# Causal mixing and a gated projection in token blocks: blocks taken in pairs, the second with its stages in reverse order

## The chip, the cores and the metric

The kernel runs on one core of one Trainium2 chip. The metric is the device time of one execution in microseconds; before the change it is 393.89 us, the median of three runs (393.89 to 394.47).

## The reference

`x` is 8 sequences of 4224 tokens with 192 channels. In the first step each of 8 heads (24 channels each) is a causal sum over 7 tokens, with softmaxed weights. The second step computes, on the result, a gate (a causal convolution over 5 tokens for each channel, then a sigmoid) and a value (a 192 x 192 projection), multiplies them, and projects again with 192 x 192 weights:

```python
w = softmax(weight)                                  # (8, 7), per head
x1[s] = sum_k w[h, k] * x[s - 6 + k]                 # head h of each channel
gate = sigmoid(sum_k conv_w[k] * x1[s - 4 + k])      # 5 taps per channel
out = (gate * (x1 @ w_val)) @ w_out                  # (8, 4224, 192), float32
```

## The kernel before

The tokens are worked on in two halves side by side. Channels lie on partitions: 128 of the 192 channels of each half fill one tile part `x1` (two halves, index q = 0 and 1), and the 64 channels left over of both halves together fill 128 partitions of `x2`.

*Superblocks and convolution units.* 14 superblocks (groups) of 2, 3 or 5 windows hold the tokens. The first step is a matmul with a band matrix. `conv_unit` does four windows of it into one PSUM bank (`pc`, line 310), ACT evicts the bank to `e` (line 319), and `scatter` sends it by DMA into `x1` and `x2` of the group. There are 114 units, and units for a group run two groups ahead. `todo[n]` says how many run with block n: 5 in blocks 3 and 4, then 4, 3, 3 repeating, 2 in each of the blocks 26 to 31, none later.

*Blocks.* The second step goes by blocks of 302 to 502 tokens per half; there are 36, of 448 columns (blocks 2 to 7, 32 and 33) or 502 (blocks 8 to 31), with smaller ones at both ends. For a block n:

- the gate: `gate_open` (ACT, line 382) writes the first tap into PSUM, `gate_taps` (DVE, line 389) adds the four others, and `gate_close` (ACT, line 402) writes the sigmoid to SBUF. Part 0 (`pa`, the 128 channels, two banks) and part 1 (`pb`, the 64 left over, one bank) are separate. The sigmoids go to `g1` and `g2`, with two buffers each.
- `split` (x) and `split_gated1`, `split_gated2` (the product): ACT casts to a rounded high part, POOL subtracts it to get a low part (lines 410, 411 for part 1, 418, 419 for part 2).
- the projections `v` and `o`, each into three banks: q = 0, 1 for the 128 channels of each half, 2 for the 64 of both. `diagonal` (line 445) and `main` (line 455) use the whole 128 x 128 array, `columns` (line 483) uses 128 x 64 tiles in f32, `rows` (line 468) uses 64 x 128 tiles. Products are written as three matmuls of high and low parts, except in `columns`.
- `gated` (DVE, line 502) multiplies v's bank by the gate, in place in `g1` or `g2`; `project` (ACT, line 518) evicts o's bank, and after the last one the block is sent out by DMA.

*The order.* It is written out by hand: each engine executes its instructions in the order of the program text. The loop over n does the v projection of block n, the o projection of block n - 1, most of the gate of n + 1 and the opening of the gate of n + 2, in the order `diagonal` v and o, `main` v, `columns` v and o, `rows` v and o, `main` o, and then the units of `todo[n]`.

*PSUM.* Of eight banks `pa` has two, `pb` one, and five rotate among `pc`, `v` and `o`.

Of the kernel before, what the change touches and what calls it, by code (L numbers as in the profile page):

```python
# [7 lines left out]
F32 = mybir.dt.float32  # L8
# [5 lines left out]
PSUM = bass.MemoryType.PSUM  # L14
# [3 lines left out]
NH, KW, HC, KG = 8, 7, 24, 5  # L18
# [50 lines left out]
STEPS = []  # L69
# [5 lines left out]
N = len(STEPS)  # L75
# [16 lines left out]
LAG = 2  # L92
BY_POOL, EARLY, AHEAD = 3, 4, 6
WARM = 11, 5, 14

SOON = {2: (0, 2), 3: (1, 3), 4: (3, 5), 5: (5, 8)}


@with_exitstack
def kernel(  # L100
# [9 lines left out]
    nc = tc.nc  # L110
# [6 lines left out]
    pp = ctx.enter_context(tc.tile_pool(name="pp", bufs=2))  # L117
    op = ctx.enter_context(tc.tile_pool(name="op", bufs=3))
    ps_g = ctx.enter_context(tc.tile_pool(name="ps_g", bufs=1, space=PSUM))
    ps_h = ctx.enter_context(tc.tile_pool(name="ps_h", bufs=1, space=PSUM))  # L120
    ps = ctx.enter_context(tc.tile_pool(name="ps", bufs=5, space=PSUM))
    ctx.enter_context(
        tc.manual_schedule(engines={ENG.PE, ENG.Activation, ENG.DVE, ENG.Pool, ENG.SP})
    )

    loads = []
    o = 0
    for g, n in enumerate(NJS):  # L130
        k = PER_LOAD[n]
# [20 lines left out]
    def load_x(upto):  # L152
        while loaded[0] < min(upto, len(loads)):
            i = loaded[0]
            loaded[0] += 1
            g, hs, o = loads[i]
            f = len(hs) * NJS[g] * M
            t = xtiles[i] = xin.tile([WK, XW], F32, tag="x", name=f"x_{i}")
            nc.sync.dma_start(t[:, :f], xw[o : o + WK * f].rearrange("(p f) -> p f", f=f))
# [13 lines left out]
    def scratch(n, i):  # L173
        o = scr_at[i]
        scr_at[i] += n
        return scr[i][:, o : o + n].bitcast(I32)

    raw = {}
    for name, ap, n, i in (("wv", wv, 2 * D + 2 * KG, 2), ("wo", wo, 2 * D, 1)):
        t = scratch(2 * n, i)  # L180
# [16 lines left out]
    nc.scalar.activation(warm, one, AF.Exp)  # L197

    def zeros(k):
        pw = ps.tile([128, 512], F32, tag="p", name="pw")  # L200
        for i in range(k):
            nc.tensor.matmul(pw[:M, :WIN], lhsT=zero[:, :M], rhs=zero[:, M:], start=True, stop=True)

# [90 lines left out]
    first_unit = [next(i for i, u in enumerate(units) if u[0] == g) for g in range(NG)] + [len(units)]  # L294

    def conv_unit(u):
        g, q, ws = units[u]
        n = NJS[g]
        if u == first_unit[g]:
            x1s[g] = xp.tile([128, 2 * XB], F32, tag="x1", name=f"x1_{g}")  # L300
            x2s[g] = xp.tile([128, XC], F32, tag="x2", name=f"x2_{g}")
        if ws[0] == (0, 0):
            es[g, q] = ep.tile([M, 4 * NMAX * WIN], F32, tag="e", name=f"e_{g}_{q}")
        e = es[g, q]
        pc = ps.tile([128, 512], F32, tag="p", name=f"pc_{u}")
        for k, (hi, j) in enumerate(ws):
            h = QUADS[q][hi]
            i, at = home[g, h]
            c = (at * n + j) * M
            nc.tensor.matmul(  # L310
                pc[:M, k * WIN : (k + 1) * WIN],
                lhsT=xtiles[i][:, c : c + M],
                rhs=band[:, 4 * q + hi, :],
                start=True,
                stop=True,
            )
        a = (ws[0][0] * n + ws[0][1]) * WIN
        w = len(ws) * WIN
        nc.scalar.copy(e[:, a : a + w], pc[:M, :w])  # L319
        done = [hi for hi, j in ws if j == n - 1]  # L320
        for hi in done:
            h = QUADS[q][hi]
            i, at = home[g, h]
            last = at == len(loads[i][1]) - 1
            if last and g >= BY_POOL:
                load_x(allowed(i))
            scatter(g, h, e[:, hi * n * WIN : (hi + 1) * n * WIN])
            if last and g < BY_POOL:
                load_x(allowed(i))
# [40 lines left out]

    accs, g1s, g2s, xs, pr, ots, banks = {}, {}, {}, {}, {}, {}, {}

    def gate_open(n, i):
        if n >= N:
            return
        m = STEPS[n][2]
        if i == 0:
            acc = ps_g.tile([128, 2, 512], F32, tag="pa", name=f"pa_{n}")[:, :, :m]
        else:
            acc = ps_h.tile([128, 512], F32, tag="pb", name=f"pb_{n}")[:, :m]  # L380
        accs[n, i] = acc
        nc.scalar.mul(acc, views(n, 0)[i], cwt[:, i, 0:1])  # L382

    def gate_taps(n, i, k0=1, k1=KG):
        if n >= N:
            return
        acc = accs[n, i]
        for k in range(k0, k1):
            nc.vector.scalar_tensor_tensor(  # L389
                out=acc, in0=views(n, k)[i], scalar=cwt[:, i, k : k + 1],  # L390
                in1=acc, op0=ALU.mult, op1=ALU.add,
            )

    def gate_close(n, i):
        if n >= N:
            return
        m = STEPS[n][2]
        if i == 0:
            dst = g1s[n] = gp.tile([128, 2, MB], F32, tag="g1", name=f"g1_{n}")[:, :, :m]
        else:  # L400
            dst = g2s[n] = gp.tile([128, MB], F32, tag="g2", name=f"g2_{n}")[:, :m]
        nc.scalar.activation(dst, accs.pop((n, i)), AF.Sigmoid)  # L402

# [16 lines left out]
    HALVES = (slice(0, 64), slice(64, 128))  # L422

    def bank(what, n, q):
        t = ps.tile([128, 512], F32, tag="p", name=f"{what}_{n}_{q}")[:, : STEPS[n][2]]
        banks[what, n, q] = t
        return t

    def operands(what, n):
        return (w_val, *xs[n, 1], *xs[n, 2]) if what == "v" else (w_out, *pr[n, 1], *pr[n, 2])  # L430
# [4 lines left out]
    def ok(n):  # L435
        return 0 <= n < N

    def diagonal(what, n):
        if not ok(n):
            return  # L440
        acc = bank(what, n, 2)
        w, _, _, h2, l2 = operands(what, n)
        r = slice(W22, W22 + 128)
        for i, (a, b) in enumerate(parts(w, h2, l2)):
            nc.tensor.matmul(acc, lhsT=a[:, r], rhs=b, start=(i == 0), stop=False)  # L445

    def main(what, n, q):
        if not ok(n):
# [23 lines left out]
    def columns(what, n):  # L472
        if not ok(n):
            return
        m = STEPS[n][2]
        acc = banks[what, n, 2]
        w = w_val if what == "v" else w_out
        x = views(n)[0] if what == "v" else g1s[n]
        cuts = [m * i // 4 for i in range(5)]
        for i in range(4):  # L480
            c = slice(cuts[i], cuts[i + 1])
            for q, p in enumerate(HALVES):
                nc.tensor.matmul(  # L483
                    acc[p, c], lhsT=w.f[:, W12 : W12 + 64], rhs=x[:, q, c],
                    start=False, stop=(i == 3),
                )

    def split(n):
# [9 lines left out]
    def gated(n, q):  # L498
        if not ok(n):
            return  # L500
        v = g1s[n][:, q] if q < 2 else g2s[n]
        nc.vector.tensor_tensor(out=v, in0=banks.pop(("v", n, q)), in1=v, op=ALU.mult)  # L502

    def split_gated1(n):
        if ok(n):
# [6 lines left out]
    def project(n, q):  # L512
        if not ok(n):
            return
        m = STEPS[n][2]
        if n not in ots:
            ots[n] = op.tile([128, 3 * MB], F32, tag="ot", name=f"ot_{n}")
        nc.scalar.copy(ots[n][:, q * m : (q + 1) * m], banks.pop(("o", n, q)))  # L518
        o = 3 * sum(s[2] for s in STEPS[:n])
        if n == LAST:  # L520
            nc.sync.dma_start(out[:, o + q * m : o + (q + 1) * m], ots[n][:, q * m : (q + 1) * m])
        elif q == 1:
            nc.sync.dma_start(out[:, o : o + 3 * m], ots[n][:, : 3 * m])
# [7 lines left out]
    done = [0]  # L531

    def conv(k):
        for _ in range(k):
            if done[0] < len(units):
                conv_unit(done[0])
                done[0] += 1

    todo = [0] * (N + 1)
    for g in range(LAG, NG):  # L540
        a, b = SOON.get(g) or (first[g - LAG], first[g - 1])
        k = first_unit[g + 1] - first_unit[g]
# [15 lines left out]
    split(0)  # L558
    w_out.join(nc.gpsimd)
    gate_taps(0, 0)  # L560
    conv(1)
    gate_close(0, 0)
    gate_open(1, 0)
    w_out.cast(nc.gpsimd)
    conv(first_unit[LAG] - done[0])
    gate_taps(0, 1)
    gate_close(0, 1)
    gate_open(1, 1)

    for n in range(N + 1):  # L570
        diagonal("v", n)
        gate_taps(n + 1, 0, 1, 3)
        split(n + 1)
        diagonal("o", n - 1)
        main("v", n, 0)
        main("v", n, 1)
        gate_taps(n + 1, 0, 3, KG)
        columns("v", n)
        gated(n, 2)
        gate_close(n + 1, 0)  # L580
        gate_open(n + 2, 0)
        columns("o", n - 1)
        split_gated2(n)
        project(n - 1, 2)
        rows("v", n)
        gated(n, 0)
        gated(n, 1)
        rows("o", n - 1)
        split_gated1(n)
        main("o", n - 1, 0)  # L590
        gate_taps(n + 1, 1)
        project(n - 1, 0)
        main("o", n - 1, 1)
        project(n - 1, 1)
        conv(todo[n])
        gate_close(n + 1, 1)
        gate_open(n + 2, 1)


# [89 lines left out]
```

## Time and profile before

| | |
|---|---|
| median of three runs | 393.89 us |
| the profiled execution's own time | 394.33 us |
| its span (first to last instruction) | 392.5 us |
| mean granted TensorE clock | 0.994 |
| PE busy | 377.6 us (96%) |
| DVE busy | 342.6 us (87%) |
| ACT busy | 323.3 us (82%) |
| POOL busy | 255.0 us (65%) |

PE is the matmuls, PEld the weight loads that overlap them, DVE the vector engine, ACT the scalar engine, POOL the GpSimd engine, SP the engine that issues most DMAs. In rows of instructions the columns are start and duration in us, engine, line, operation, output and inputs, shapes, count, and in brackets the idle time before and what ended it. A row with a count covers several instructions in sequence, so its duration is that of all of them. In rows of waits the columns are the engine that waits, whom for, total us, number of waits, longest.

### The profile page before, as it was taken

To read this page: it belongs to the slowest core of one execution; us is meant where nothing else is said; L and a number is where in the kernel's file an instruction comes from. 1 tells how busy PE (TensorE), PEld (TensorE's weight loads), DVE (VectorE), ACT (ScalarE), POOL (GpSimd) and SP (SyncE) were. 2 spreads that over 40 slices of the span, in tenths; PEclk is the share of its full clock that TensorE was granted. 3 is DMA by queue.
4 is the path that set the end of the run, shared out by engine and by line. 5 is a ranking of instruction groups with operands and counts; after the bars stand their busy time and mean duration, and the time that the engine had idled before them with its cause. 6 is when DMAs were issued, how large, how long until landed. Compare 5 with 4: busy or idle time off the path is not lost.

```text
span 392.5 us, 8623 instructions
## 1 busy us (share of the span) xinstructions
PE 377.6 (96%) x3204; PEld 320.5 (82%) x3204; DVE 342.6 (87%) x424; ACT 323.3 (82%) x525; POOL 255.0 (65%) x177
## 2 busy tenths in 40 slices
PE   8977999999999999999999999999999999999895
PEld 7965989988888888888888888888888777788684
DVE  3798798887998998998999899899899999999970
ACT  7467888978988888888889888888888888887863
POOL 1876865566666665666665676666566776766771
PEclk9998999999999999999999999999999999999999
DMA  8866769998888687867867758768887644334224
GB/s 294 243 167 200 216 199 300 225 270 247 259 249 218 206 261 229 234 201 242 234 193 245 223 193 256 211 193 264 248 233 218 219 151 154 114 123 144 80 90 160
DMA packets 38209, 82.49 MB, mean 210 GB/s; under 512 B 4856, under 2 KB 17528, under 8 KB 38168
## 3 DMA queue, kind: packets, MB, share of 16 engines
q1 hardware_dynamic: 36720, 79.90, 66.7%
q0 software_dynamic: 896, 1.31, 1.5%
q10 hardware_dynamic: 552, 0.73, 0.6%
q8 instruction: 25, 0.41, 0.5%
q14 instruction: 16, 0.13, 0.1%
HBM read 29.34 MB, written 26.00 MB: 141 GB/s over the span
## 4 chain that ended last, share of the span: by engine, by line
PE 71%; DVE 11%; DMA 6%; ACT 5%; POOL 2%; issue 2%; SPq 1%; ACTq 0%; DVEq 0%; POOLq 0%
PE pc L310 18%; PE o L455 10%; PE v L455 9%; PE v L483 7%; PE v L468 6%; PE o L483 6%; DVE pa L389 5%; PE o L468 5%; PE o L445 5%; PE v L445 4%; DVE pb L389 3%; DMA x<-xw 2%; DMA x<-e 2%; DVE g L502 2%; DMA scr<-wv 2%
## 5 line engine op out<-in xcount | busy, mean ns | idle before, releaser
L389 DVE SCALAR_TENSOR_TENSOR pa<-x,cwt,pa 128x1004 f32<-128x1004 f32 (+5 forms) x144 | 172.9, 1201 | 7.2 <-ACT pa L382 2.2
L411 POOL TENSOR_TENSOR xl<-x,xh 128x1004 fp32r<-128x1004 f32 (+5 forms) x36 | 74.8, 2077 | 73.9 <-ACT xh L410 65.3
L310 PEld LDWEIGHTS pc<-band,x 128*120 128x120 f32 x912 | 101.1, 184 | 7.1 <-ACT e L319 1.4
L310 PE MATMUL pc<-band,x 128*120 128x122 f32 x912 | 102.7, 269 | 3.5 <-DMA x<-xw 1.9
L389 DVE SCALAR_TENSOR_TENSOR pb<-x,cwt,pb 128x502 f32<-128x502 f32 (+5 forms) x144 | 102.3, 710 | 3.8
L502 DVE TENSOR_TENSOR g<-v,g 128x502 f32<-128x502 f32 (+5 forms) x108 | 65.9, 643 | 24.7 <-PE v L468 17.0
L411 POOL TENSOR_TENSOR pl<-g,ph 128x1004 fp32r<-128x1004 f32 (+5 forms) x36 | 79.3, 2204 | 9.1 <-ACT ph L410 6.8
L402 ACT ACTIVATE g<-pa 128x1004 f32<-128x1004 f32 (+5 forms) x36 | 34.5, 958 | 42.8 <-DVE pa L389 22.7
L419 POOL TENSOR_TENSOR pl<-g,ph 128x502 fp32r<-128x502 f32 (+5 forms) x36 | 42.9, 1191 | 38.0 <-ACT ph L418 38.0
L319 ACT COPY e<-pc 120x488 f32<-120x488 f32 x114 | 58.8, 588 | 3.6 <-PE pc L310 3.4
L518 ACT COPY ot<-o 128x502 f32<-128x502 f32 (+5 forms) x108 | 55.9, 551 | 1.5 <-PE o L455 1.0
L382 ACT ACTIVATE pa<-x,cwt 128x1004 f32<-128x1004 f32 (+5 forms) x36 | 37.8, 1050 | 8.3 <-DMA x<-e 6.2
L419 POOL TENSOR_TENSOR xl<-x,xh 128x502 fp32r<-128x502 f32 (+5 forms) x36 | 41.8, 1162 | 0.0
L483 PEld LDWEIGHTS v<-x,wvf 128*64 128x64 f32 x576 | 29.4, 138 | 11.9 <-issue 11.3
L483 PE MATMUL v<-x,wvf 128*64 128x125 f32 (+4 forms) x576 | 37.5, 272 | 0.0
L410 ACT CAST ph<-g 128x1004 fp32r<-128x1004 f32 (+5 forms) x36 | 35.1, 976 | 1.5 <-DVE g L502 1.5
L483 PE MATMUL o<-g,wof 128*64 128x125 f32 (+4 forms) x576 | 35.6, 264 | 0.0
L410 ACT CAST xh<-x 128x1004 fp32r<-128x1004 f32 (+5 forms) x36 | 34.6, 962 | 0.0
L483 PEld LDWEIGHTS o<-g,wof 128*64 128x64 f32 x576 | 30.9, 136 | 0.1
L455 PE MATMUL o<-ph,woh 128*128 128x502 f32 (+5 forms) x72 | 30.8, 428 | 0.0
L455 PE MATMUL v<-xl,wvh 128*128 128x502 f32 (+5 forms) x72 | 27.4, 381 | 0.8 <-POOL xl L411 0.8
L455 PE MATMUL v<-xh,wvl 128*128 128x502 f32 (+5 forms) x72 | 27.4, 381 | 0.0
(75 smaller groups left out, 572.4 us busy)
## 6 DMA issues: line engine op xcount, KB each, us to landing
x<-xw SPq DMA_DIRECT2D x64, 300.0 KB
out<-ot SPq DMA_DIRECT2D x24, 753.0 KB
x<-e SPq DMA_DIRECT2D x40, 285.9 KB
x<-xw SPq DMA_DIRECT2D x20, 360.0 KB
out<-ot SPq DMA_DIRECT2D x8, 672.0 KB
x<-e SPq DMA_DIRECT2D x32, 141.6 KB
x<-e SPq DMA_DIRECT2D x25, 171.6 KB
x<-e SPq DMA_DIRECT2D x16, 94.4 KB
```

Of the source, the lines that this page charges most:

```text
L310: nc.tensor.matmul(pc[:M, k * WIN : (k + 1) * WIN], lhsT=xtiles[i][:, c : c + M], rhs=band[:, 4 * q + hi, :], start=True, stop=True,)
L319: nc.scalar.copy(e[:, a : a + w], pc[:M, :w])
L382: nc.scalar.mul(acc, views(n, 0)[i], cwt[:, i, 0:1])
L389: nc.vector.scalar_tensor_tensor(out=acc, in0=views(n, k)[i], scalar=cwt[:, i, k : k + 1], in1=acc, op0=ALU.mult, op1=ALU.add,)
L410: nc.scalar.copy(h, x)
L411: nc.gpsimd.tensor_tensor(out=l, in0=x, in1=h.bitcast(F32), op=ALU.subtract)
L419: nc.gpsimd.tensor_tensor(out=l, in0=x, in1=h.bitcast(F32), op=ALU.subtract)
L455: nc.tensor.matmul(acc, lhsT=a[:, r], rhs=b[:, q], start=(fresh and i == 0), stop=(not fresh and i == 2))
L468: nc.tensor.matmul(acc, lhsT=a[p, r], rhs=b[p], start=(fresh and i == 0), stop=(not fresh and i == 2))
L483: nc.tensor.matmul(acc[p, c], lhsT=w.f[:, W12 : W12 + 64], rhs=x[:, q, c], start=False, stop=(i == 3),)
L502: nc.vector.tensor_tensor(out=v, in0=banks.pop(("v", n, q)), in1=v, op=ALU.mult)
L518: nc.scalar.copy(ots[n][:, q * m : (q + 1) * m], banks.pop(("o", n, q)))
```

## The change

From block 4 on, blocks are done in pairs (a, b = a + 1) by a new function `pair`; blocks 0 to 3 and the last, empty step keep the old order (`plain`). In the pair, block a has the order `diagonal`, `main`, `columns`, `rows`, with the o stages of block a - 1 beside v's, and block b the order `rows`, `columns`, `main`, `diagonal`, with the o stages of block a; the `diagonal` and `main` of o for block a come at the end, with one unit ahead of each. The units of block a now stand at the pair's beginning. The gates are interleaved by hand: pb of both blocks is opened in the pair before, three taps of pa of block a + 2 are added in the middle of the pair and its last tap at the beginning of the next.

The separate buffer of `pb` goes; `pc`, `v`, `o`, `pb` and the warming-up tile share six banks. The program hands out the bank that was given back first (`take`, `give`).

In the prologue all three remaining units of group 1 are done ahead of `gate_close(0, 0)`, instead of one ahead and two after it.

```diff
-    ps_h = ctx.enter_context(tc.tile_pool(name="ps_h", bufs=1, space=PSUM))
-    ps = ctx.enter_context(tc.tile_pool(name="ps", bufs=5, space=PSUM))
+    ps = ctx.enter_context(tc.tile_pool(name="ps", bufs=1, space=PSUM))
...
+    free, held = list(range(6)), {}
+
+    def take(key, name):
+        held[key] = free.pop(0)
+        return ps.tile([128, 512], F32, tag=f"p{held[key]}", name=name)
+
+    def give(key):
+        free.append(held.pop(key))
...
     gate_taps(0, 0)
-    conv(1)
+    conv(first_unit[LAG] - done[0])
     gate_close(0, 0)
     gate_open(1, 0)
     w_out.cast(nc.gpsimd)
-    conv(first_unit[LAG] - done[0])
...
+    def pair(a):
+        b = a + 1
+        gate_taps(a, 0)
+        k = todo[a]
+        conv(min(k, 1))
+        gate_close(a, 0)
+        gate_taps(a, 1)
+        gate_open(a + 1, 0)
+        conv(max(0, k - 1))
+        gate_close(a, 1)
+        gate_open(a + 1, 1)
+        gate_taps(a + 1, 1)
+        split(a + 1)
+        diagonal("v", a)
+        main("v", a, 0)
+        main("v", a, 1)
+        diagonal("o", a - 1)
+        gate_close(a + 1, 1)
+        main("o", a - 1, 0)
+        main("o", a - 1, 1)
+        gate_taps(a + 1, 0)
+        columns("v", a)
+        gated(a, 2)
+        gate_close(a + 1, 0)
+        columns("o", a - 1)
+        split_gated2(a)
+        project(a - 1, 2)
+        rows("v", a)
+        gated(a, 0)
+        gated(a, 1)
+        gate_open(a + 2, 0)
+        rows("o", a - 1)
+        project(a - 1, 0)
+        project(a - 1, 1)
+        split_gated1(a)
+        gate_taps(a + 2, 0, 4)
+
+        rows("v", b)
+        rows("o", a)
+        columns("v", b)
+        columns("o", a)
+        split(a + 2)
+        main("v", b, 0)
+        main("v", b, 1)
+        diagonal("v", b)
+        gated(b, 0)
+        gate_open(a + 2, 1)
+        gated(b, 1)
+        split_gated1(b)
+        gated(b, 2)
+        split_gated2(b)
+        k = todo[b]
+        conv(min(k, 1))
+        diagonal("o", a)
+        project(a, 2)
+        gate_open(a + 3, 1)
+        conv(min(max(0, k - 1), 1))
+        main("o", a, 0)
+        project(a, 0)
+        conv(min(max(0, k - 2), 1))
+        main("o", a, 1)
+        project(a, 1)
+        conv(max(0, k - 3))
```

The helpers are adapted: a gate part is opened and closed only once even if the text asks twice, `gate_taps(n, i, end)` adds the taps that are still missing up to `end`, and `diagonal`, `rows`, `columns` and `main` start a bank where they come first and end it where they come last.

More of the change, by code (lines that the diff above doesn't have):

```diff
@@ L94 @@
 WARM = 11, 5, 14
+PAIRED = 4
 SOON = {2: (0, 2), 3: (1, 3), 4: (3, 5), 5: (5, 8)}
@@ L199, in zeros @@
     def zeros(k):
-        pw = ps.tile([128, 512], F32, tag="p", name="pw")
+        pw = take("pw", "pw")
+        give("pw")
         for i in range(k):
@@ L304, in conv_unit @@
         e = es[g, q]
-        pc = ps.tile([128, 512], F32, tag="p", name=f"pc_{u}")
+        pc = take("pc", f"pc_{u}")
         for k, (hi, j) in enumerate(ws):
@@ L319, in conv_unit @@
         nc.scalar.copy(e[:, a : a + w], pc[:M, :w])
+        give("pc")
         done = [hi for hi, j in ws if j == n - 1]
@@ L371 @@
     accs, g1s, g2s, xs, pr, ots, banks = {}, {}, {}, {}, {}, {}, {}
+    opened, tapped, closed = set(), {}, set()
     def gate_open(n, i):
-        if n >= N:
+        if n >= N or (n, i) in opened:
             return
+        opened.add((n, i))
+        tapped[n, i] = 1
         m = STEPS[n][2]
@@ L379, in gate_open, with gate_taps @@
         else:
-            acc = ps_h.tile([128, 512], F32, tag="pb", name=f"pb_{n}")[:, :m]
+            acc = take(("pb", n), f"pb_{n}")[:, :m]
         accs[n, i] = acc
         nc.scalar.mul(acc, views(n, 0)[i], cwt[:, i, 0:1])
-    def gate_taps(n, i, k0=1, k1=KG):
+    def gate_taps(n, i, end=KG):
         if n >= N:
             return
-        acc = accs[n, i]
-        for k in range(k0, k1):
+        while tapped[n, i] < end:
+            k = tapped[n, i]
+            tapped[n, i] += 1
+            acc = accs[n, i]
             nc.vector.scalar_tensor_tensor(
@@ L394, in gate_close @@
     def gate_close(n, i):
-        if n >= N:
+        if n >= N or (n, i) in closed:
             return
+        closed.add((n, i))
+        assert tapped[n, i] == KG
         m = STEPS[n][2]
@@ L402, in gate_close @@
         nc.scalar.activation(dst, accs.pop((n, i)), AF.Sigmoid)
+        if i == 1:
+            give(("pb", n))
     def split1(pool, tag, n, x):
@@ L424, in bank @@
     def bank(what, n, q):
-        t = ps.tile([128, 512], F32, tag="p", name=f"{what}_{n}_{q}")[:, : STEPS[n][2]]
+        t = take((what, n, q), f"{what}_{n}_{q}")[:, : STEPS[n][2]]
         banks[what, n, q] = t
@@ L440, in diagonal @@
             return
-        acc = bank(what, n, 2)
+        fresh = (what, n, 2) not in banks
+        acc = bank(what, n, 2) if fresh else banks[what, n, 2]
         w, _, _, h2, l2 = operands(what, n)
@@ L444, in diagonal @@
         for i, (a, b) in enumerate(parts(w, h2, l2)):
-            nc.tensor.matmul(acc, lhsT=a[:, r], rhs=b, start=(i == 0), stop=False)
+            nc.tensor.matmul(
+                acc, lhsT=a[:, r], rhs=b, start=(fresh and i == 0), stop=(not fresh and i == 2)
+            )
     def main(what, n, q):
@@ L475, in columns @@
         m = STEPS[n][2]
-        acc = banks[what, n, 2]
+        fresh = (what, n, 2) not in banks
+        acc = bank(what, n, 2) if fresh else banks[what, n, 2]
         w = w_val if what == "v" else w_out
@@ L484, in columns @@
                     acc[p, c], lhsT=w.f[:, W12 : W12 + 64], rhs=x[:, q, c],
-                    start=False, stop=(i == 3),
+                    start=(fresh and i == 0), stop=(not fresh and i == 3),
                 )
@@ L502, in gated @@
         nc.vector.tensor_tensor(out=v, in0=banks.pop(("v", n, q)), in1=v, op=ALU.mult)
+        give(("v", n, q))
     def split_gated1(n):
@@ L518, in project @@
         nc.scalar.copy(ots[n][:, q * m : (q + 1) * m], banks.pop(("o", n, q)))
+        give(("o", n, q))
         o = 3 * sum(s[2] for s in STEPS[:n])
@@ L568, with plain @@
     gate_open(1, 1)
-    for n in range(N + 1):
+    def plain(n):
         diagonal("v", n)
-        gate_taps(n + 1, 0, 1, 3)
+        gate_taps(n + 1, 0, 3)
         split(n + 1)
@@ L576 @@
         main("v", n, 1)
-        gate_taps(n + 1, 0, 3, KG)
+        gate_taps(n + 1, 0)
         columns("v", n)
@@ L597 @@
         gate_open(n + 2, 1)
+    def pair(a):
[60 more added lines that the diff above has]
+        conv(max(0, k - 3))
+    n = 0
+    while n <= N:
+        if n < PAIRED or n + 1 >= N:
+            plain(n)
+            n += 1
+        else:
+            pair(n)
+            n += 2
 def kernel(x, weight, moe_w_val, moe_conv_w, moe_w_out):
```

## The prediction

> **What bounds the kernel now.** I read the page's busy times first, then the list of waits, then the busy time by stretch, and last the order of time on each engine in one middle block.
>
> ```profile
> PE 377.6 (96%) x3204; PEld 320.5 (82%) x3204; DVE 342.6 (87%) x424; ACT 323.3 (82%) x525; POOL 255.0 (65%) x177
> 159.20:169.50 10.30, 10.30 (x89) 8.68 (x87) 9.74 (x12) 8.98 (x15) 6.91 (x5) 1.00 0.66 195
> ACT g L402 <- PE o L483: 14.3, 12, 1.4
> PEld o L455 <- issue: 11.8, 35, 0.4
> PEld v L483 <- issue: 11.3, 33, 0.4
> ```
>
> The second row is a stretch in the middle (length, then busy time of PE, weight load, DVE, ACT, POOL, granted clock, DMA share, GB/s). PE is busy for the whole of it; DVE follows at 9.74 of 10.30. PE sets the pace, but DVE has little room. What PE does in that block:
>
> ```profile
> 159.11 0.47 PE L445 MATMUL v<-xh,wvh 128*128 128x502 f32 x1
> 159.42 0.39 PE L445 MATMUL v<-xh,wvl 128*128 128x502 f32 x1
> ...
> 161.69 0.38 PE L455 MATMUL v<-xl,wvh 128*128 128x502 f32 x1
> 162.01 1.08 PE L483 MATMUL v<-x,wvf 128*64 128x125 f32 x16
> 162.92 1.03 PE L483 MATMUL o<-g,wof 128*64 128x125 f32 x16
> 163.88 0.49 PE L468 MATMUL v<-xh,wvh 64*128 64x502 f32 x2
> 164.22 0.41 PE L468 MATMUL v<-xh,wvl 64*128 64x502 f32 x2
> ...
> 165.56 0.49 PE L455 MATMUL o<-ph,woh 128*128 128x502 f32 x1
> 165.89 0.39 PE L455 MATMUL o<-ph,wol 128*128 128x502 f32 x1
> ...
> 167.02 2.68 PE L310 MATMUL pc<-band,x 128*120 128x122 f32 x24
> 169.47 0.47 PE L445 MATMUL v<-xh,wvh 128*128 128x502 f32 x1
> ```
>
> A block with three convolution units lasts 169.47 - 159.11 = 10.36 us, two of them 20.72. A full matmul starts 0.23 after the one before it, a group of 16 column matmuls takes 0.91, a unit 2.45 / 3 = 0.82. Where the tiling changes, the step is longer: full to 64 columns 0.32 (0.09 over), columns to 64 rows 0.96 and then 0.34 (0.05 + 0.11 over), rows to full 0.33 after the first (0.10 over, and about 0.1 ahead of it). The two rows "<- issue" of the waits are those places. After the f32 convolution the first step is 0.31 (0.08 over).
>
> The other two engines that matter, DVE first, then ACT:
>
> ```profile
> 158.87 5.17 DVE L389 SCALAR_TENSOR_TENSOR pa<-x,cwt,pa 128x1004 f32<-128x1004 f32 x4
> 163.95 0.67 DVE L502 TENSOR_TENSOR g<-v,g 128x502 f32<-128x502 f32 x1
> 164.97 1.27 DVE L502 TENSOR_TENSOR g<-v,g 128x502 f32<-128x502 f32 x2 [0.35 <-PE v L468]
> 166.16 3.08 DVE L389 SCALAR_TENSOR_TENSOR pb<-x,cwt,pb 128x502 f32<-128x502 f32 x4
> 169.15 5.17 DVE L389 SCALAR_TENSOR_TENSOR pa<-x,cwt,pa 128x1004 f32<-128x1004 f32 x4
> ```
>
> ```profile
> 164.16 1.01 ACT L402 ACTIVATE g<-pa 128x1004 f32<-128x1004 f32 x1 [1.25 <-DVE pa L389]
> 165.20 1.10 ACT L382 ACTIVATE pa<-x,cwt 128x1004 f32<-128x1004 f32 x1
> 166.24 0.60 ACT L418 CAST ph<-g 128x502 fp32r<-128x502 f32 x1
> 166.74 0.57 ACT L518 COPY ot<-o 128x502 f32<-128x502 f32 x1
> 167.21 1.03 ACT L410 CAST ph<-g 128x1004 fp32r<-128x1004 f32 x1
> 168.14 1.06 ACT L518 COPY ot<-o 128x502 f32<-128x502 f32 x2
> 169.08 1.52 ACT L319 COPY e<-pc 120x488 f32<-120x488 f32 x3
> 170.45 0.64 ACT L402 ACTIVATE g<-pb 128x502 f32<-128x502 f32 x1
> 171.75 1.01 ACT L410 CAST xh<-x 128x1004 fp32r<-128x1004 f32 x1
> 172.66 0.61 ACT L418 CAST xh<-x 128x502 fp32r<-128x502 f32 x1
> ```
>
> From start to start a pa tap is 1.27 (four 5.08), four pb taps 2.99, a product 0.60 (0.67 to its end): 5.08 + 2.99 + 3 x 0.60 = 9.9 us of DVE per block. In this order the way round through ACT costs DVE nothing: after the last pa tap (164.04) ACT closes that gate and opens the next until 166.30, while DVE does three products and four pb taps up to 169.15.
>
> **What the change saves.** Per pair PE changes tiling four times and not six: full, columns, rows over the block's end, columns, full. Saved are one rows-to-full (0.2) and one full-to-columns (0.09), about 0.3. Against it the evictions between the o matmuls cut the convolution into pieces, so there are four f32-to-fp32r steps per pair and not two: 2 x 0.08 = 0.16. Net 0.15 to 0.4 us of PE per pair. Instruction counts stay the same on all engines and queues, so nothing else is saved there.
>
> **What it adds: a ring of waits.** All else is an in-order walk through `pair` with the durations above, three units per block. Call the blocks a and b, the pair before a' and b'. Six shared banks are held at two places, so the list makes PE wait. Following the list by hand: b's first unit takes the bank that gated(b,1) frees (v(b,0)'s goes to the next pb), b's second unit the bank of the first, and o(a-1,1) the bank that closing pb of b frees. Start at PE's first unit of b':
>
> 1. PE: unit 0.82, diagonal o 0.77; the second unit waits for the first one's eviction, which on ACT is behind the two casts of the gated products of b' (0.93, 0.50) and takes 0.57 itself, so it starts at 2.1 and not at 1.6. Then unit, main o, unit, main o, and a's first unit: 2.1 + 0.82 + 0.77 + 0.82 + 0.77 + 0.82, and its end 0.17 later: 6.3.
> 2. ACT, in order behind that unit's eviction (1.37 / 3 = 0.46): close pa of a 1.04, open pa of b 1.04, two evictions 0.91, close pb of a 0.6, split b 0.91 + 0.6, close pb of b 0.63: 6.2. DVE meanwhile idles: its last tap of a and both sets of pb taps end 7.7 us after the ring's start, and pa of b is open only at 8.9; its four taps then end at about 14.0.
> 3. PE: main o(a-1,1), held at its bank, 0.68, mode change 0.09, columns v 0.91, columns o(a-1) to their end 1.03: 2.7. PE has waited about 1 us at the bank.
> 4. ACT: closing pa of b needs a g1 buffer, of which there are two, and the old one is read by columns o(a-1). The row "ACT g L402 <- PE o L483" shows this wait in the kernel before; here it comes at 15.4 and decides over the taps (14.0). Close 0.93, cast 0.50, eviction 0.47, open pa of a+2 1.10: 3.0. DVE has only gated(a,2), (a,0), (a,1) meanwhile (1.8 us), then idles.
> 5. DVE: three taps of pa of a+2 3.81, gated(b,0) 0.60, gated(b,1) 0.67: 5.1, and the bank for b's first unit is free: the ring is closed.
>
> The sum is 6.3 + 6.2 + 2.7 + 3.0 + 5.1 = 23.3 and five handoffs between engines of about 0.08 (164.04 to 164.16 is one of 0.12): **23.7 us a pair against 20.72.** The cover that is gone is that of the pa way round: before, 5 us of other DVE work lay over it, here 1.8, twice per pair (steps 2 and 4). PE's own 20.3 of work then has some 3.4 us of idle time, in pieces of 1 us and less: at o(a-1,1), at rows v(b) (its second bank is that of the eviction of o(a-1,2)), and at b's first and second unit. POOL's work per pair (2 x 6.91 in the stretch above) and the DMAs, whose order on SP is that of the units as before, lie beside this; the third rows-o(a) matmul waits for POOL's split of the gated product, but no longer than for the bank ahead of it.
>
> With four units in b the ring grows by a unit, as the kernel before does; with four in a by one eviction (0.46) where before it was a unit (0.82); with two in each it shrinks by 1.4 to 22.3, where before DVE's 9.9 a block held. For a mean: the stretch from block 6 to block 32 is 13 pairs.
>
> ```profile
> 86.83 0.45 PE L445 MATMUL v<-xh,wvh 128*128 128x448 f32 x1
> 355.49 0.45 PE L445 MATMUL v<-xh,wvh 128*128 128x448 f32 x1
> 372.69 0.39 PE L445 MATMUL v<-xh,wvh 128*128 128x500 f32 x1
> ```
>
> These are the starts of blocks 6, 32 and 34. Before, 355.49 - 86.83 = 268.7, plus 1.6 since my ring begins ahead of b's units (four in block 5, two in block 31): 270.3. By the ring: one pair of 448 columns 23.1; nine pairs 3 x (23.7 + 24.5 + 24.2) = 217.2; one with three units in b' and two in a 23.2; two with two and two 44.6: 308.1. The difference is **+37.8**.
>
> The edges: pair 4 starts with both its gates closed, so DVE has a light half and its second half begins some 2 us earlier than before, with one block's o left to do (-2). From block 32 no unit is left; the ring without evictions gives 20.3 for pair 32 against 17.2 + 1.6 = 18.8 before (+1.5). The end, from pair 34 on, does the o left over, with the same ring on smaller tiles (+2). Bounds of the three together, by the smallest and largest wait in them, -2 to +5; taken +1.5.
>
> **The prologue.** Two evictions go ahead of closing gate 0. ACT was idle 1.73 us just there, waiting for the taps (first row below), and two evictions are 0.9, so they cost nothing; their scatters leave earlier.
>
> ```profile
> 22.04 0.68 ACT L402 ACTIVATE g<-pa 128x608 f32<-128x608 f32 x1 [1.73 <-DVE pa L389]
> 31.03 1.01 ACT L382 ACTIVATE pa<-x,cwt 128x896 f32<-128x896 f32 x1 [2.73 <-DMA x<-e]
> 20.00:41.00 21.00, 15.59 (x142) 13.03 (x141) 18.72 (x29) 15.25 (x29) 15.76 (x20) 0.92 0.65 176
> ```
>
> The wait of 2.73 for group 1's tokens (second row) stands ahead of everything ACT does next. It goes, and next late is DVE (18.72 of 21.00 busy, third row). Bounds -2.7 and +1 (the evictions delaying the close); taken -2.5.
>
> **Sum.** +37.8 + 1.5 - 2.5 = +36.8 on the profiled execution's own 394.33 is 431; the median of the runs is 0.4 lower, so about **430 us**.
>
> [...] In the stretch 20 to 41, where PE was busy for 15.59 of 21.00, the granted clock was 0.92; in the stretch of 10.30 us above it was 1.00. With PE at 20.3 of 23.7 the clock could fall. [...]
>
> **The rivals.**
> - Only DVE's own loop binds, and PE's bank waits are shorter than I walk them: taps 1.27 + 2 x 2.99 + 5.08, handoff 0.12, close, cast, eviction, open 3.0, handoff 0.1, taps 3.81, products 1.8 = 21.2 a pair. Thirteen pairs are 276, +6; with the edges and the prologue 399. For it speaks that each of its links is a plain data dependence with a row; against it that the banks in steps 1 and 3 are given out by a fixed list. Without the bank of step 1 alone PE goes straight on, the ring is about 1 us shorter, 417.
> - Faster: PE stays the bound and the fewer mode changes show. 0.15 to 0.4 x 16 pairs and 2.5 in the prologue: about 388. It decides if DVE's idle time between the taps of b and those of a+2 is below 20.3 - 19.8 = 0.5 us a pair; I find 1.4 even when the g1 buffer is free in time (3.2 for ACT's four steps and the handoffs, less 1.8 of products). [...]
> - No change: the ring is 20.8 by chance. It would take 3 us of slack in steps 2 and 4, of which no row shows any.
> [...]
>
> **How the numbers follow.** The forecast of 430 (own range 417 to 439) has 0.62; DVE's loop alone, 396 to 415, 0.21; the clock 0.05; faster 0.08; no change within 0.2% (about what these runs can tell apart: 393.89 to 394.47) 0.04. So faster 0.08, same 0.04, slower 0.88. The range 400 to 439 leaves out faster, no change and the clock (0.17) and a little of DVE's loop.
>
> **What would show it.** Right: in a middle pair of the changed kernel the starts of two second-half diagonals of v lie 23 to 24.5 us apart; PE has idle time of about 1 us ahead of main o(a-1,1) put down to ACT closing pb; DVE idles over 1 us ahead of the three pa taps, put down to ACT opening pa, and about 1 us ahead of b's four; ACT waits for PE's columns o ahead of the second pa close; PE's busy share falls to some 88%, clock 1.00; the 2.73 at the fourth pa opening is gone. Wrong: PE still over 95% busy in the middle, or no wait of PE for a bank, or a DVE wait for ACT below 0.5 us a pair.

## The result and the profile after

The changed kernel takes 432.4 us (median of four runs, 431.3 to 433.8) against 394.0: **9.9% slower, ratio 1.0989 (1.0959 to 1.1019).** 430 was forecast. The profiled execution has a span of 429.5 us, 37.0 more than before.

The page's busy times, the middle stretch of the windows, and the waits (before, PE's share was 96%, and the only wait of 14 us or more of these kinds was ACT's for PE's columns o):

```profile
PE 391.6 (91%) x3204; PEld 319.8 (74%) x3204; DVE 343.8 (80%) x424; ACT 324.4 (76%) x525; POOL 252.4 (59%) x177
60.00:330.00 270.00, 253.61 (x2043) 205.60 (x2041) 220.25 (x254) 212.11 (x334) 152.58 (x91) 1.00 0.75 211
ACT g L424 <- PE o L511: 37.6, 14, 2.9
DVE pa L409 <- ACT pa L400: 32.1, 31, 2.2
PEld o L482 <- ACT g L424: 15.0, 16, 1.2
PEld pc L323 <- DVE g L530: 12.1, 15, 1.5
PEld v L495 <- ACT ot L547: 10.8, 16, 0.7
PEld pc L323 <- ACT e L332: 9.5, 14, 0.7
```

Every engine executes as many of these instructions as before, and DVE and ACT are busy for about as long (343.8 us where it was 342.6, 324.4 where it was 323.3). PE's busy time is 14.0 us longer for the same 3204 matmuls; about half of that lies in the convolution (109.9 us where it was 102.7), which is now cut into more pieces. What is new, or far longer, are waits that come 14 to 16 times, once per pair, or 31 times, twice per pair. They name the links of the ring: ACT's close waits for columns o, DVE's taps for ACT's opening of pa, PE's main o for ACT's closing of pb, b's first unit for DVE's product, rows v for the eviction of o, b's second unit for the first one's eviction. The granted clock in the middle is 1.00.

One pair with three units per block, all engines in order of time:

```profile
200.75 1.10 PE L323 MATMUL pc<-band,x 128*120 128x122 f32 x8 [0.31 <-DVE g L530]
202.80 1.10 PE L323 MATMUL pc<-band,x 128*120 128x122 f32 x8 [0.26 <-ACT e L332]
205.95 2.68 PE L323 MATMUL pc<-band,x 128*120 128x122 f32 x24
206.99 0.56 ACT L332 COPY e<-pc 120x488 f32<-120x488 f32 x1 [0.26 <-PE pc L323]
207.45 1.01 ACT L424 ACTIVATE g<-pa 128x1004 f32<-128x1004 f32 x1
209.64 5.18 DVE L409 SCALAR_TENSOR_TENSOR pa<-x,cwt,pa 128x1004 f32<-128x1004 f32 x4 [1.21 <-ACT pa L400]
212.36 0.61 ACT L424 ACTIVATE g<-pb 128x502 f32<-128x502 f32 x1
213.02 0.50 PE L482 MATMUL o<-ph,woh 128*128 128x502 f32 x1 [0.53 <-ACT g L424]
214.81 1.03 PE L511 MATMUL o<-g,wof 128*64 128x125 f32 x16
215.89 1.01 ACT L424 ACTIVATE g<-pa 128x1004 f32<-128x1004 f32 x1 [2.92 <-PE o L511]
217.01 0.40 PE L495 MATMUL o<-pl,woh 64*128 64x502 f32 x2
217.24 0.39 PE L495 MATMUL v<-xh,wvh 64*128 64x502 f32 x1
217.76 1.12 ACT L400 ACTIVATE pa<-x,cwt 128x1004 f32<-128x1004 f32 x1
217.93 0.49 PE L495 MATMUL v<-xh,wvh 64*128 64x502 f32 x1 [0.29 <-ACT ot L547]
218.91 3.88 DVE L409 SCALAR_TENSOR_TENSOR pa<-x,cwt,pa 128x1004 f32<-128x1004 f32 x3 [0.81 <-ACT pa L400]
222.70 1.85 DVE L530 TENSOR_TENSOR g<-v,g 128x502 f32<-128x502 f32 x3
224.01 1.10 PE L323 MATMUL pc<-band,x 128*120 128x122 f32 x8 [0.28 <-DVE g L530]
```

Read it as a ring. b's first unit starts at 200.75; the eviction of a's first unit at 206.99 (step 1, 6.24 us); main o(a-1,1) gets its bank at 213.02 (step 2, 6.03); the close of b's pa starts at 215.89, 0.05 after columns o end (step 3, 2.87); the three taps start at 218.91 (step 4, 3.02); and the next pair's first unit follows at 224.01 (step 5, 5.10). That is 23.26 us against 20.72 before. At 217.01 to 217.24 PE crosses from block a to block b without a surcharge (a step of 0.23, like those before it), so a change of tiling is really saved there (0.2 by the rows of the kernel before). Right behind it PE waits for a bank (the row at 217.93), so the time doesn't show it.

### The profile page after: what moved, and what is told of

Read it like the earlier page. It is cut to its first block, busy times and chain, and to the rows that moved or that the text cites. A ratio compares the mean times of both kernels' runs of the same rounds, so it can differ in the third digit from the quotient of the medians.

```text
span 429.5 us, 8659 instructions
## 1 busy us (share of the span) xinstructions
PE 391.6 (91%) x3204; PEld 319.8 (74%) x3204; DVE 343.8 (80%) x424; ACT 324.4 (76%) x525; POOL 252.4 (59%) x177
## 4 chain that ended last, share of the span: by engine, by line
ACT 31%; PE 27%; DVE 19%; DMA 11%; issue 6%; SPq 3%; POOL 1%; ACTq 0%; POOLq 0%; DVEq 0%
DVE pa L409 15%; PE pc L323 12%; DMA x<-xw 8%; ACT g L424 7%; ACT pa L400 6%; PE o L482 6%; ACT e L332 5%; DVE g L530 4%; ACT ph L434 3%; DMA x<-e 3%; PE v L511 3%; ACT ph L442 3%; PE o L511 3%; SPq L362 2%; ACT pb L400 2%
## 5 line engine op out<-in xcount | busy, mean ns | idle before, releaser
L323 PEld LDWEIGHTS pc<-band,x 128*120 128x120 f32 x912 | 102.8, 184 | 28.0 <-DVE g L530 12.1
L323 PE MATMUL pc<-band,x 128*120 128x122 f32 x912 | 109.9, 273 | 12.5 <-DVE g L530 5.9
L409 DVE SCALAR_TENSOR_TENSOR pb<-x,cwt,pb 128x502 f32<-128x502 f32 (+5 forms) x144 | 101.0, 711 | 8.1 <-ACT pb L400 4.2
L530 DVE TENSOR_TENSOR g<-v,g 128x502 f32<-128x502 f32 (+5 forms) x108 | 65.0, 642 | 29.1 <-PE v L495 18.0
L332 ACT COPY e<-pc 120x488 f32<-120x488 f32 x114 | 62.4, 565 | 14.9 <-PE pc L323 13.3
L547 ACT COPY ot<-o 128x502 f32<-128x502 f32 (+5 forms) x108 | 57.4, 555 | 5.0 <-PE o L511 1.1
L511 PE MATMUL v<-x,wvf 128*64 128x125 f32 (+4 forms) x576 | 37.7, 273 | 0.0
L400 ACT ACTIVATE pb<-x,cwt 128x502 f32<-128x502 f32 (+5 forms) x36 | 23.8, 661 | 17.9 <-DVE g L530 17.9
L511 PE MATMUL o<-g,wof 128*64 128x125 f32 (+4 forms) x576 | 36.1, 267 | 0.0
L434 ACT CAST xh<-x 128x1004 fp32r<-128x1004 f32 (+5 forms) x36 | 35.7, 991 | 0.0
L482 PE MATMUL v<-xh,wvh 128*128 128x502 f32 (+5 forms) x72 | 30.2, 419 | 0.9
```

Source lines behind the costliest of these rows:

```text
L323: nc.tensor.matmul(pc[:M, k * WIN : (k + 1) * WIN], lhsT=xtiles[i][:, c : c + M], rhs=band[:, 4 * q + hi, :], start=True, stop=True,)
L409: nc.vector.scalar_tensor_tensor(out=acc, in0=views(n, k)[i], scalar=cwt[:, i, k : k + 1], in1=acc, op0=ALU.mult, op1=ALU.add,)
L434: nc.scalar.copy(h, x)
L482: nc.tensor.matmul(acc, lhsT=a[:, r], rhs=b[:, q], start=(fresh and i == 0), stop=(not fresh and i == 2))
L511: nc.tensor.matmul(acc[p, c], lhsT=w.f[:, W12 : W12 + 64], rhs=x[:, q, c], start=(fresh and i == 0), stop=(not fresh and i == 3),)
```

## The experiments

Ratios are to the kernel before, run on the same chip, with their 95% intervals. Of the edits within the pair the first three take away one link each.

**A third g1 buffer.** 1.0703 (1.0674 to 1.0731), 421.2 us.

```diff
+    gp1 = ctx.enter_context(tc.tile_pool(name="gp1", bufs=3))
-            dst = g1s[n] = gp.tile([128, 2, MB], F32, tag="g1", ...
+            dst = g1s[n] = gp1.tile([128, 2, MB], F32, tag="g1", ...
```

> The changed kernel with three buffers for g1 and not two. Theory (ring): closing pa of b no longer waits for columns o(a-1); in the traced pair it came at 15.14 us after the ring's start and DVE's taps ended at 14.07, so it comes at about 14.2 and the pair loses 0.9 to 1.0 us: 23.3 becomes about 22.4 and the whole about 418 us (415 to 423). Rival (another wait, the bank of o(a-1,1) or PE's own order, sets the pair): unchanged, 430 to 434.

11.2 us less than the changed kernel, and 22.49 a pair in the trace (195.89 to 218.38). The close of b's pa now waits for DVE's taps:

```profile
210.00 1.01 ACT L425 ACTIVATE g<-pa 128x1004 f32<-128x1004 f32 x1 [1.88 <-DVE pa L410]
```

**pb of b closed ahead of split(b).** 1.0736 (1.0707 to 1.0765), 422.5 us.

```diff
         gate_taps(a + 1, 1)
+        gate_close(a + 1, 1)
         split(a + 1)
...
         diagonal("o", a - 1)
-        gate_close(a + 1, 1)
```

> The changed kernel with pb of b closed ahead of split(b) and not behind it, so that o(a-1,1)'s bank is free 1.5 us earlier on ACT. Theory (ring): PE's wait there, 0.7 us in the traced pair, goes, columns o(a-1) end 0.7 us earlier and so does closing pa of b: 22.6 us a pair, about 422 us (418 to 426). Rival (DVE's and ACT's own loop, without PE, sets the pair): unchanged, 430 to 434.

9.9 us less, and 22.45 a pair (196.76 to 219.21). PE's wait at main o(a-1,1) is gone: it starts 0.24 after the matmul before it, where in the changed kernel that step was 0.93 (212.09 to 213.02).

```profile
208.34 0.39 PE L482 MATMUL o<-ph,woh 128*128 128x502 f32 x1
```

So the wait cost about what it took in the trace. DVE's and ACT's own loop, whose steps this edit doesn't shorten, was not the limit.

**pa of a closed and pa of b opened ahead of a's first unit.** 1.0896 (1.0852 to 1.0941), 428.1 us.

```diff
-        conv(min(k, 1))
         gate_close(a, 0)
         gate_taps(a, 1)
         gate_open(a + 1, 0)
-        conv(max(0, k - 1))
+        conv(k)
```

> The changed kernel with closing pa of a and opening pa of b ahead of a's first unit and not behind it. Theory (ring through PE): pa of b opens about 0.8 us earlier and DVE's four taps with it, but closing pa of b still waits for columns o(a-1), which wait for the same ACT work as before, so the time stays at 432 us (429 to 434). Rival (DVE's and ACT's own loop sets the pair): 0.8 us a pair, about 420.

4.3 us less, more than expected of the ring and far from the 12 of DVE's loop. The trace shows why:

```profile
201.23 1.10 PE L323 MATMUL pc<-band,x 128*120 128x122 f32 x8 [0.34 <-DVE g L530]
213.16 0.49 PE L482 MATMUL o<-ph,woh 128*128 128x502 f32 x1 [0.32 <-ACT g L424]
224.15 1.10 PE L323 MATMUL pc<-band,x 128*120 128x122 f32 x8 [0.30 <-DVE g L530]
```

The pair takes 22.92. ACT no longer stands idle for 0.26 ahead of the eviction of a's first unit (the row at 206.99 above), so pb closes, and PE goes on, 11.93 us after the start and not 12.27. From there to the next pair's start both kernels take 10.99, so it gave nothing that DVE's taps started earlier.

**Two taps in the middle, two at the beginning.** 1.1035 (1.0995 to 1.1074), 433.8 us.

```diff
-        gate_taps(a + 2, 0, 4)
+        gate_taps(a + 2, 0, 3)
```

> The changed kernel with two taps of pa of a+2 in the middle of the pair and two at the next one's beginning, not three and one. Theory (two ways of nearly the same length end at b's first unit): DVE's products could start 1.27 us earlier, but main v(b,1) ends only 0.2 us ahead of where they start now, so about 0.2 us a pair: 430 us (426 to 433). Rival (DVE's loop alone sets the pair): 1.27 us a pair, about 413.

No gain over the changed kernel (the intervals overlap), and just above the expected 426 to 433. The traced pair is 0.20 shorter, as expected (199.82 to 222.88), but the whole keeps nothing of it. DVE now waits for PE where the third tap was:

```profile
198.48 2.04 DVE L530 TENSOR_TENSOR g<-v,g 128x502 f32<-128x502 f32 x3 [0.93 <-PE v L482]
```

So two ways of nearly the same length end at b's first unit, and shortening DVE's alone is worth little.

**The three edits together.** 1.0419 (1.0385 to 1.0453), 409.6 us.

> The changed kernel with three of its waits taken away together: three buffers for g1, pb of b closed ahead of split(b), and pa of a closed and pa of b opened ahead of a's first unit. Theory: pa of b opens at 8.1 us of the ring, its taps end at 13.2, the close follows at 13.3 and the rest of the ring as now (8.1 us): about 21.5 us a pair, 406 us (401 to 411), more than the two single edits together (11 and 10 us). Rival (the first unit's bank or PE's own chain to the eviction of o(a-1,2) holds the pair at 22.5): 419.

```profile
190.87 1.10 PE L324 MATMUL pc<-band,x 128*120 128x122 f32 x8
212.42 1.10 PE L324 MATMUL pc<-band,x 128*120 128x122 f32 x8
```

The pair takes 21.55 us, as the ring said, and the whole 22.8 us less than the changed kernel: these three waits account for 60% of its loss.

**Diagonal o(a) ahead of b's first unit, and then a tap left out.** 1.0451 (1.0412 to 1.0489), 410.7 us, and 1.0410 (1.0384 to 1.0437), 409.1 us.

```diff
+        diagonal("o", a)
+        project(a, 2)
         conv(min(k, 1))
-        diagonal("o", a)
-        project(a, 2)
         gate_open(a + 3, 1)
```

```diff
         b = a + 1
-        gate_taps(a, 0)
+        tapped[a, 0] = KG
```

> The kernel with three waits taken away, and in it diagonal o(a) ahead of b's first unit, so that PE has work while DVE frees that unit's bank. Theory: PE's waits at b's first and second unit (0.25 and 0.4 us of a ring of 21.55) go, but DVE's way round (taps, close, cast, eviction, open, three taps, products: 21.2 to 21.4) is then the longest; 0.2 us a pair, about 406 us (403 to 408). Rival (PE is now the bound): 0.6 us a pair, about 400.

> The same, with the last pa tap of block a left out in every pair from the second on (its output lacks that tap), so DVE has 18.6 us a pair and not 19.9. Theory (DVE's way round sets the pair): 0.4 to 1.2 us a pair, until the way through PE and ACT (about 20.6 to 21) holds: 391 to 401, middle 397. Rival (DVE does not matter any more): 406.

Both missed: neither gained. The first moved a wait instead of taking it away, and the second shows that DVE's own loop is not the limit. The first row is of the run with the diagonal first, the others of the run with a tap left out:

```profile
200.63 5.18 DVE L410 SCALAR_TENSOR_TENSOR pa<-x,cwt,pa 128x1004 f32<-128x1004 f32 x4 [0.21 <-ACT pa L401]
193.53 1.10 PE L324 MATMUL pc<-band,x 128*120 128x122 f32 x8 [0.61 <-ACT ot L548]
199.54 5.18 DVE L410 SCALAR_TENSOR_TENSOR pa<-x,cwt,pa 128x1004 f32<-128x1004 f32 x4 [1.38 <-ACT pa L401]
```

b's second unit, now without a wait for DVE at the first, waits 0.61 for a bank that ACT's eviction of o frees. With the tap DVE waits 0.21 for pa of b, without it 1.38: the tap is gone, the wait is longer by as much, and the pair takes 21.54 where it took 21.56. This tap is off the longest way; DVE's pa taps of b, which neither run shortens, are still waited for by ACT (1.43 us ahead of b's close).

**The same tap left out of the kernel before.** 0.9977 (0.9959 to 0.9994), 392.7 us.

```diff
-        gate_taps(n + 1, 0, 3, KG)
+        gate_taps(n + 1, 0, 3, KG - (n % 2 == 1 and n >= 5))
```

> The kernel before, with the last pa tap left out in every second block from block 6 on (the same omission). Theory (PE sets the pace except in the blocks with two units or none): middle pairs unchanged at 20.7 us, some 0.6 us less in the last five pairs, 390 to 392. Rival (DVE sets the pace too): over 1 us a pair, below 380.

Hardly anything, as for a kernel that PE paces; the gain expected at the end did not come in full (390 to 392 was expected).

**No pairs.** 1.0320 (1.0294 to 1.0345), 406.2 us.

```diff
-PAIRED = 4
+PAIRED = 99
```

> The changed kernel with all blocks in the old order: what is left of the change are the six shared banks and the prologue edit. Theory (the waits come from the order in the pair): within 2 us of the prologue edit alone, 394 to 398 us, middle blocks with three units still 10.3 to 10.4 us. Rival (sharing the banks makes PE wait in any order): over 405 us.

The rival was right about the size: without any pair the kernel is some 12 us slower than before. These are not 12 of the changed kernel's 38 us, since there only blocks 0 to 3 keep the old order. Middle blocks with three units take 10.71 (156.11 to 166.82) and not 10.36:

```profile
PEld pc L323 <- ACT ot L547: 18.9, 31, 0.9
156.11 0.47 PE L470 MATMUL v<-xh,wvh 128*128 128x502 f32 x1
163.66 0.57 ACT L547 COPY ot<-o 128x502 f32<-128x502 f32 x1
164.28 2.78 PE L323 MATMUL pc<-band,x 128*120 128x122 f32 x24 [0.15 <-ACT ot L547]
166.82 0.47 PE L470 MATMUL v<-xh,wvh 128*128 128x502 f32 x1
```

In nearly every block with units (31 waits) the first unit waits for the eviction of o's third part (163.66 to 164.23). The list takes it for the bank that has been free the longest, because the program text gives it back ahead of v's first two. In time those two come first.

**The list's order mended, no pairs.** 1.0033 (1.0010 to 1.0055), 394.2 us.

```diff
-PAIRED = 4
+PAIRED = 99
...
     def give(key):
-        free.append(held.pop(key))
+        if key[0] == "o" and key[2] == 2:
+            late.append(held.pop(key))
+        else:
+            free.append(held.pop(key))
+
+    late = []
...
         gated(n, 1)
+        free.extend(late)
+        late.clear()
```

> All blocks in the old order with six shared banks, as in the run without pairs, but the bank of o's third part goes into the free list behind those of v's first two, which DVE has read before ACT has evicted o. Theory (the 11.8 us that the run without pairs lost come from the list alone: each block's first unit waits 0.3 us for the eviction of o's third part, of whose bank the list thinks that it has been free for longer): middle blocks back at 10.3 to 10.4 us, the whole 394 to 397 us. Rival (having pb among the six takes a bank away, whatever the order): 404 to 407.

```profile
158.64 0.48 PE L475 MATMUL v<-xh,wvh 128*128 128x502 f32 x1
168.99 0.48 PE L475 MATMUL v<-xh,wvh 128*128 128x502 f32 x1
```

Blocks are back at 10.35 us. So it was not pb's share of the six banks, only which bank comes next. The 0.3% that are left are no more than the prologue edit costs by itself (next run).

**The prologue edit alone, in the kernel before.** 1.0026 (1.0002 to 1.0050), 394.4 us.

```diff
-    conv(1)
+    conv(first_unit[LAG] - done[0])
     gate_close(0, 0)
     gate_open(1, 0)
     w_out.cast(nc.gpsimd)
-    conv(first_unit[LAG] - done[0])
```

> The kernel before with the prologue edit alone (three units ahead of closing gate 0). Theory, from the trace after: the fourth pa opening comes about 1.3 us earlier, but PE's idle time ahead of the first o diagonal grows from 2.7 to 3.4 us, PE stays at half clock for about 3.4 us longer, and block 2 starts about 1 us later; PE sets the pace from there on, so the whole is about 395 us (394.3 to 396). Rival, the prediction's term: 2.5 us faster, 391.5.

It costs about 1 us (0.1 to 2.0) and gains nothing. The time is the expected one; the trace, of an execution of 396.2 us, doesn't show the expected way. The three units wait 3.10 for their input and then run at a granted clock of 0.50 (in the window from 21 to 24), 5.21 us for what takes 2.75 in the kernel before, at 1.00. ACT's evictions wait for them, so ACT comes to the fourth pa opening only at 30.81 and finds the tokens there. PE's pause ahead of the first o diagonal is 0.21 and not 3.4, and ACT and PE wait for DVE a little later:

```profile
19.33 5.21 PE L310 MATMUL pc<-band,x 128*120 128x122 f32 x24 [3.10 <-DMA x<-xw]
38.47 0.92 ACT L402 ACTIVATE g<-pa 128x896 f32<-128x896 f32 x1 [1.97 <-DVE pa L389]
38.78 0.42 PE L468 MATMUL o<-ph,woh 64*128 64x304 f32 x1 [2.38 <-DVE g L502]
```

## Why the prediction was right

**The ring.** Its five steps were put at 6.3, 6.2, 2.7, 3.0 and 5.1 us and are 6.24, 6.03, 2.87, 3.02 and 5.10. The sum of 23.7 is 0.4 too long because the handoffs were added to steps that held them already. With four units in b or in a the pairs take 24.1 and 23.75, with two in each 21.7 to 22.0, again some 0.4 under the forecast's 24.5, 24.2 and 22.3. Taking links away one by one moved the time by about what each wait took in the trace, and three together gave the ring that the same sum gives (21.5 expected, 21.55 measured). So three links are shown by edits: the g1 buffer, the bank of o(a-1,1) and ACT's queue ahead of it. The bank of b's first unit rests on the rows, since the run that put the diagonal ahead of that unit moved its wait on to the second. The waits within the steps are smaller than the prediction named them: PE's ahead of main o(a-1,1) is 0.53 and not about 1, DVE's ahead of the three taps 0.81 and not over 1, and PE's busy share is 91% and not 88%.

**Where the 37.0 us of span lie**, by four rows of the two traces:

```profile
60.03 4.36 PE L310 MATMUL pc<-band,x 128*120 128x122 f32 x40
```

```profile
61.74 8.66 PE L323 MATMUL pc<-band,x 128*120 128x122 f32 x80 [0.17 <-ACT ot L547]
83.28 0.89 PE L323 MATMUL pc<-band,x 128*120 128x122 f32 x6 [0.32 <-DVE g L530]
385.77 1.10 PE L323 MATMUL pc<-band,x 128*120 128x122 f32 x8
```

The first is of before (the units after block 3), the others of after: block 3's units, and b's first units of the pairs with blocks 4 and 30.

- Up to block 3's units: +1.7, forecast -2.5.
- Pair 4: 83.28 - 61.74 = 21.5, where the kernel before took 23.6 to the same place (four units of 0.81 ahead of 86.83): -2.0, as forecast.
- Thirteen pairs: 385.77 - 83.28 = 302.5 against 270.3: **+32.2**, forecast +37.8. The excess is those 0.4 us a pair.
- From there to the end: 43.7 against 38.6, +5.1, forecast +3.5. What the end is made of was not taken apart.

So the forecast hit 430 with two errors that cancelled: the ring 5.6 too dear, the edges 5.8 too cheap together. The mechanism was right; that the sum came so close is luck.

**The prologue** is the term that failed, in sign. The wait of 2.73 at the fourth pa opening was to go, and in the changed kernel it did not. The scatters left earlier (SP had issued its four by 23.6 and not 27.5), but group 1's tokens were there only 1.3 us earlier, at 29.74 and not 31.03; ACT itself came 0.8 earlier, and 2.20 of the wait stayed (first row). Ahead of the first o diagonal PE stood idle for longer, 3.44 us where before it was 2.68 (second row), now for a bank that an eviction frees and no longer for its operand. The forecast also gave no price to the list of banks in blocks 0 to 3, which keep the old order: there PE's units wait three times for an eviction of o, as in the run without pairs, and these 1.3 us (third row) are most of the +1.7.

```profile
29.74 1.01 ACT L400 ACTIVATE pa<-x,cwt 128x896 f32<-128x896 f32 x1 [2.20 <-DMA x<-e]
32.23 0.62 PE L470 MATMUL o<-ph,woh 128*128 128x304 f32 x1 [3.44 <-ACT e L332]
PE pc L323 <- ACT ot L547: 1.3, 3, 0.7
```

After that pause the granted clock was 0.50 for longer, about 6.8 us where it was 3.4 in the kernel before: it is the number after the five busy times, of the kernel before and then of the changed one.

```profile
30.00:33.00 3.00, 0.55 (x2) 0.30 (x2) 1.78 (x3) 1.97 (x4) 0.52 (x1) 0.95 0.79 285
33.00:36.00 3.00, 2.76 (x18) 2.34 (x19) 2.89 (x4) 2.97 (x7) 3.00 (x5) 0.50 0.14 43
36.00:39.00 3.00, 3.00 (x47) 2.74 (x44) 2.51 (x5) 2.58 (x4) 3.00 (x6) 0.98 0.96 259
```

```profile
30.00:33.00 3.00, 0.77 (x3) 0.77 (x4) 2.31 (x3) 3.00 (x7) 1.81 (x2) 0.65 0.25 98
33.00:36.00 3.00, 3.00 (x28) 2.70 (x28) 2.44 (x3) 2.28 (x5) 3.00 (x6) 0.50 0.41 89
36.00:39.00 3.00, 3.00 (x34) 2.67 (x31) 1.44 (x4) 1.79 (x2) 2.98 (x5) 0.71 1.02 256
```

The longer half clock can't be put down to the change: the kernel before with a tap left out has the old prologue, and in its trace a pause of 2.23 us is followed by some 6.1 us of PE at half pace, as the last section shows. Nor is the 1.7 a fixed price: in the seven other traces of kernels with pairs the units after block 3 start at 61.0 to 64.1 us. What the edit by itself costs is the 1 us of its own run.

**The rivals.** DVE's own loop (399) is refuted: the moved tap, the tap left out (in the kernel with three waits taken away) and the earlier opening of pa each shortened it, and only the last gained, by PE's way. The clock did not fall in the middle: 1.00 with PE at 94% of the stretch; the longest of PE's waits that repeat once per pair is 1.5 us. That it would hold with PE at 20.3 of 23.7 was the author's estimate, shown by no row of before. In the prologue it fell to 0.50, with a pause of 2.68 us in the kernel before and of 3.44 us in the changed one, as the last section shows. The faster case had its mechanism (fewer mode changes) and not its condition.

**What the prediction lacked** is the share of the list. It followed the list inside the pair but did not ask whether its rule, longest free in the program's order, is right in time; the 12 us between the runs with and without the mended list, in the old order (406.2 and 394.2), show that it isn't. How much of the pair's own loss would go with a mended list there was not tried. Nor was a version found that beats the kernel before; the nearest with pairs is 4.2% slower.

## What to carry to other kernels

When work is reordered to save on one engine, write out the ring through all in-order queues and shared buffers before counting the saving: here 0.3 us a pair on PE was paid for with 2.5, and a third gate buffer, an earlier close of pb and an earlier opening of pa together took back 1.7 of it. Shortening a ring helps only at a link that every one of its parallel ways passes: take links away singly and see which move the time. A list that hands out the buffer "free the longest" must be ordered by when readers finish, not by where the release stands in the text.

## What the runs showed of the hardware

In the kernel before PE paused for 2.68 us, up to 32.45, after a stretch in which it was busy for about half of the time (1.77 of the 3 us from 27 to 30), and the granted clock was 0.50 for about 3.4 us (by windows of 0.25 us, from 32.7 to 36.1; 0.95, 0.50 and 0.98 in the three stretches of 3 us). In the changed kernel PE paused for 3.44 us at the same place, up to 32.23, and the granted clock was 0.50 for about 6.8 us (from 30.9 to 37.7; 0.65, 0.50 and 0.71).

The longer pause is not the reason. In the kernel before with a tap left out a pause of 2.23 us was followed by PE at half pace from 31.84 to 37.96, 6.1 us: its matmuls of 302 columns start 0.25 us apart there (33.17 to 34.43), and those of 304 columns 0.14 behind it. In the run without pairs a pause of 3.60 us was followed by about 3.3 us of half pace, an estimate: the 24 convolution matmuls behind it took 4.16 us up to the next start (20.42 to 24.58), where 24 in the kernel before took 2.51 at a clock of 1.00, and the steps after that are again 0.14. The kernel before and the changed one also differ in when PE came back to work: 0.3 us ahead of the clock's fall in the one, 1.4 us after it in the other. That the order of these two is the reason was not tested.
